# Bias of the first four tiles by 64-row matmuls, score groups as one unit, and a new order of all units in an attention and max-out kernel

## The chip, the cores and the metric

The kernel runs on one core of a Trainium2 chip. A core has engines with queues of their own: TensorE (PE, matrix multiplies, with the loads of its weights shown apart as PEld), VectorE (DVE), ScalarE (ACT), GpSimd (POOL), and SyncE (SP), which here only issues DMAs. PE reads from SBUF and writes to PSUM. Engines wait for one another through semaphores, and each works through its own list in order. The metric is the device time of one execution in microseconds (us); smaller is better.

## The reference

Attention with a local window and a few global columns, then a feed-forward layer with a maximum over three products.

```python
# q, k, v: [4, 8, 768, 64] f32; n_global = 8, n_local = 96; w1, w2, w3: [512, 768]; w_out: [768, 512]
scores = q @ k.T / sqrt(64)
rel = pos[:, None] - pos[None, :]
is_global = pos[None, :] < 8
is_local = (rel >= 0) & (rel < 96)
dist = where(is_global & ~is_local, 96, abs(rel))
slopes = 2.0 ** (-8.0 * (arange(8) + 1) / 8)            # one per head
scores = where(is_global | is_local, scores - slopes * dist, -1e9)
a = softmax(scores)
x = (a @ v) with heads side by side                     # [4 * 768, 512]
h = maximum(maximum(x @ w1, x @ w2), x @ w3)
out = h @ w_out                                         # [3072, 512]
```

## The kernel before, in words

The 3072 rows are 24 tiles of 128 positions, six to a batch. A tile T sees the keys of a window of two 64-row halves plus eight global columns; the first tile of a batch (T = 0, 6, 12, 18) sees one key set only. Everything is written as units, and the string SCHEDULE (lines 25 to 61) lists all of them in one order. A letter names the function (the table at lines 536 to 539), the numbers are its arguments, and the last one often chooses the engine. The scheduler is manual: every engine gets its instructions in the order in which the units stand in the string, and so does SP with its DMAs. Nothing else sets the order; only semaphores and free buffers decide when an instruction starts.

The life of two tiles (a pair n): l loads q (s = 0) or k (s = 1) by DMA into one of five raw buffers, c casts it to bf16, x brings it into the transposed layout qkT (how 2, 3, 6, 7, 8 by transposes on PE with copies from PSUM by ACT or DVE; 9 by a DMA transpose issued on SP). v loads values, C casts them, and Y and V copy parts of them to where tiles of odd alignment and the global rows read them. G copies the eight global key columns beside a tile's own. Then for each tile: S multiplies keys by queries for one of two groups g of four heads (8 matmuls whose contraction is 64 rows, so that two heads use the two halves of the array) and lets ACT take the exponential into P. The bias on the distance enters in one of two ways. With how = 1 two more matmuls of 128 rows first put it into PSUM, an identity times the tile "bias" (line 299), which B has made as slope times distance for each head. With how = 0 M multiplies P on DVE by the mask wmask, an exponential that K has made (line 334). Tiles 0 to 3 and one group of tile 4 take the first way, so that DVE has no masks to multiply at the start. A multiplies P by values and DVE divides by the row sum (lines 372, 373); it takes PSUM from the score buffers sp0 or sp1, or with how = 2 from the buffers "h". T transposes the result into xT, on PE with copies, or by DMA on SP (how 4). For T = 0, 6, 12, 18 a unit Z first gathers the keys of both halves into one tile kf, so that one matmul covers 128 keys.

The feed-forward part works on chunks of 4, 2, 2, 4, 4, 4 and 4 tiles. F (chunk, f, j) does four matmuls into one of three PSUM buffers "h" (line 424); for j = 0 ACT copies the result out (line 429), for j = 1 and 2 DVE takes the maximum (lines 431, 433). O multiplies by w_out and stores a tile, E does the last chunk. w, W, o and Q load and cast weights. D puts matmuls on zeros into PE's queue. Before the loop, DVE and POOL build the distance table rbq and the identity (lines 510 to 534). The first feed-forward matmul, F0.1.0, reads xT of tiles 0 to 3.

Of the kernel before, what the change touches and what calls it, by code (L numbers as in the profile page):

```python
# [12 lines left out]
FP32 = mybir.dt.float32  # L13
# [12 lines left out]
    K7 l1.0 c1.0.2 K6 l1.1 B6.1 D0.4 D4.4 B5.1 D2.0 D5.4 K0 c0.1.1 c0.0.1 K2 D8.0 B0.1 B4.0 B1.0  # L26
    B3.0 x0.1.3 K1 K3 K5 c1.1.2 B7.0 x0.0.7 D1.1 D9.2 S1.0.1 Z0.1 B2.1 v0 C0.0.2 S1.1.1 G1.0 x1.0.8
    K4 M1.0 S0.0.1 M0.0 v1 x1.1.8 S2.1.1 S2.0.1 M2.0 C0.1.2 Y0.1.2 Y1.0.1 M1.1 V2.1 Y0.0.1 G2.1 A1.2
    S0.1.1 C1.0.2 C1.1.2 Y2.0.0 Y1.1.2 D3.1 S3.0.1 M3.0 M0.1 A0.2 S3.1.1 M3.1 l2.0 c2.0.2 x2.0.6
    T1.1 M2.1 A2.0 V3.2 T0.0 G3.0 A3.1 l2.1 c2.1.2 x2.1.6 T2.1 w0.0 W0.0.0 l3.0 w0.1 S4.0.1 M4.0  # L30
    T3.8 V4.2 W0.1.2 S4.1.0 D7.1 G4.0 w0.2 F0.1.0 F0.0.0 S5.1.0 c3.0.1 x3.0.6 M4.1 w1.0 W1.0.0
    S5.0.0 F0.1.1 W0.2.2 F0.1.2 v2 C2.0.0 C2.1.0 W2.0.1 F0.0.1 F0.0.2 M5.0 F0.3.0 F0.2.0 M5.1 Y2.1.1
    V5.1 F0.5.0 w1.1 W1.1.0 W2.1.1 F0.4.0 A4.1 A5.0 F0.5.1 T4.0 F0.4.1 w1.2 W1.2.0 l3.1 T5.1 F0.2.1
    F0.2.2 l4.0 c4.0.1 W2.2.0 F0.5.2 c3.1.0 x3.1.7 Z1.0 F0.4.2 F1.0.0 F1.2.0 l4.1 c4.1.1 S7.0.0
    S6.1.0 l5.0 x4.0.6 l5.1 o0 F1.0.1 F1.0.2 c5.0.1 M7.0 F1.3.0 F1.4.0 F1.4.1 o2 c5.1.1 x4.1.7
    S6.0.0 S7.1.0 G7.0 v3 F1.2.1 F1.2.2 F1.3.1 Q2.1 F0.3.1 M7.1 Q0.0 F1.5.0 F1.5.1 S8.0.0 x5.0.7
    S8.1.0 G8.1 C3.0.2 C3.1.1 Y4.0.1 F0.3.2 F1.5.2 A7.0 F1.4.2 F1.1.0 M6.0 x5.1.6 v5 o1 Q1.0 v4
    S9.0.0 S9.1.0 l7.0 l6.1 C5.0.1 C5.1.0 F1.1.1 F1.3.2 Y3.1.1 M8.0 F1.1.2 T7.0 v6 l6.0 M6.1 v7
    Y3.0.1 M9.0 O0.2.1 l7.1 C4.0.0 O0.0.0 G9.0 V8.1 A6.1 c7.0.1 M8.1 c6.1.1 x6.1.9 O0.3.0 C4.1.0
    Y4.1.1 O0.1.1 Y5.1.0 S10.1.0 T6.8 V9.1 M9.1 S10.0.0 O1.0.0 A8.1 M10.1 T8.4 F2.0.0 x7.0.9 G10.0  # L40
    F2.4.0 c6.0.0 l8.1 v9 l9.1 F2.0.1 F2.1.0 M10.0 F2.0.2 S11.0.0 c7.1.0 Y5.0.1 x6.0.6 S11.1.0 V10.1
    F2.1.1 M11.0 F2.4.1 C6.0.0 A9.0 F2.2.0 V11.1 l9.0 O1.1.1 S13.1.0 x7.1.6 S13.0.0 G13.0 M11.1
# [14 lines left out]
    O4.1.1 A21.1 T21.4 M23.1 M22.1 O4.0.0 V22.0 F5.4.1 F5.0.0 A23.1 T23.4 O4.3.0 A22.0 F5.4.2 F5.5.2  # L57
    F5.0.1 F5.1.1 F5.0.2 T22.4 F5.1.2 F6.3.0 F6.5.0 F6.4.0 F6.5.1 F6.4.1 F6.4.2 O5.1.0 F6.3.1 F6.1.0
    O5.3.1 F6.1.1 F6.0.0 F6.0.1 F6.0.2 O5.0.1 F6.2.0 F6.2.1 F6.3.2 O5.2.0 F6.2.2 F6.1.2 F6.5.2 E
    D6.0  # L60
"""


@with_exitstack
def kernel(
# [13 lines left out]
    nc = tc.nc  # L79
# [495 lines left out]
```

## Time and profile before

| | |
|---|---|
| runs before | 176.95 us median (176.63 to 176.96, 3 runs) |
| span of the profiled execution, first to last instruction | 174.9 us; the page gives no other time of it |
| PE, DVE, ACT, POOL busy | 169.3, 132.5, 120.1, 14.3 us |
| first feed-forward matmul starts | 21.81 us |
| last matmul ends | 171.5 us |
| transposes of q and k by PE, by DMA | 14, 10 units |
| transposes of the attention output by PE, by DMA | 12, 12 units |

Busy times are sums of instructions. The ends of matmuls are modelled in the profile, so a full PE need not be at its peak. In the timeline a row gives start and length in us, engine, line, operation, output and input, and in brackets how long the engine had waited and what released it. The chain of waits is followed back from the last instruction; its rows give start, length and what ran.

### The profile page before, as it was taken

How to read it: one execution, taken by the hardware profiler on the slowest of the kernel's cores; microseconds unless marked ns; L12 is line 12 of the kernel's file. 1: busy time of each engine (PE TensorE's matmuls, PEld its weight loads, DVE VectorE, ACT ScalarE, POOL GpSimd, SP SyncE). 2: the span in 40 equal slices, each digit the busy share in tenths (PEclk: the TensorE clock that was granted, in tenths of full speed). 3: DMA queues.
4: the chain of work that ended last, by engine and by line, in shares of the span. 5: the costliest groups of instructions: out<-in, count | busy, mean ns of one | idle time of the engine just before them, and what ended most of it. 6: DMA issues, size and time to landing. Idle time of an engine off the chain costs nothing.

```text
span 174.9 us, 4233 instructions
## 1 busy us (share of the span) xinstructions
PE 169.3 (97%) x1683; PEld 93.0 (53%) x1683; DVE 132.5 (76%) x288; ACT 120.1 (69%) x188; POOL 14.3 (8%) x25
## 2 busy tenths in 40 slices
PE   6999999999999999999999999999999999999992
PEld 2445654658684587754545545544455544444451
DVE  6668859889999999998978769995569873444510
ACT  6989999789988999999948977345594413121132
POOL 5269250000100000000000000000000000000000
PEclk9999999999999999999999999999999999999999
DMA  4999999999999999976999997563101750031205
GB/s 137 347 302 335 359 350 383 385 380 312 309 282 265 298 289 228 292 213 193 257 195 185 304 233 172 166 133 60 54 10 30 105 171 0 0 119 36 89 27 213
DMA packets 55507, 35.92 MB, mean 205 GB/s; under 512 B 18368, under 2 KB 47936, under 8 KB 55488
## 3 DMA queue, kind: packets, MB, share of 16 engines
q1 hardware_dynamic: 54304, 35.07, 73.9%
q10 hardware_dynamic: 1184, 0.59, 1.3%
q8 instruction: 13, 0.21, 0.5%
q14 instruction: 6, 0.05, 0.1%
HBM read 25.17 MB, written 6.29 MB: 180 GB/s over the span
## 4 chain that ended last, share of the span: by engine, by line
PE 94%; ACT 2%; DVE 1%; issue 1%; ACTq 0%; DVEq 0%
PE h L424 53%; PE po L439 18%; PE sp L306 7%; PE op L360 6%; PE wp L504 4%; PE tpr L261 2%; PE sp L299 2%; PE xtp L411 1%; ACT qkT L268 1%; ACT wo L496 1%; PE oph L360 1%; ACT P L317 1%; PE xtr L401 0%; PE tpp L282 0%; DVE qkT L285 0%
## 5 line engine op out<-in xcount | busy, mean ns | idle before, releaser
L424 PE MATMUL h<-xT,w 128*128 128x512 bf16 (+1 forms) x504 | 100.8, 349 | 0.0
L424 PEld LDWEIGHTS <-w 128*128 128x128 bf16 x504 | 46.7, 98 | 40.7 <-ACT w L493 0.6
L317 ACT ACTIVATE P<-sp 128x1024 bf16<-128x1024 f32 (+1 forms) x48 | 44.0, 956 | 9.2 <-PE sp L306 9.1
L429 ACT CAST h<-h 128x512 bf16<-128x512 f32 (+1 forms) x42 | 21.9, 531 | 22.1 <-PE h L424 22.1
L439 PE MATMUL po<-wo,ht 128*128 128x512 bf16 (+2 forms) x156 | 34.1, 363 | 0.0
L431 DVE TENSOR_TENSOR h<-h,h 128x512 bf16<-128x512 bf16 (+1 forms) x42 | 25.2, 605 | 10.9 <-PE h L424 8.9
L433 DVE TENSOR_TENSOR ht<-h,h 128x512 bf16<-128x512 bf16 (+1 forms) x42 | 25.5, 609 | 6.3 <-PE h L424 5.0
L334 DVE TENSOR_TENSOR P<-P,wmask 128x1024 bf16<-128x1024 bf16 x33 | 22.0, 684 | 2.0 <-ACT P L317 1.9
L439 PEld LDWEIGHTS <-ht 128*128 128x128 bf16 x156 | 14.3, 98 | 15.1 <-DVE ht L433 0.2
L448 ACT COPY ost<-po 128x512 f32<-128x512 f32 (+2 forms) x16 | 8.8, 553 | 15.8 <-PE po L439 15.3
L373 DVE TENSOR_TENSOR xb<-op,rz 128x512 bf16<-128x512 f32 x22 | 15.2, 692 | 0.8
L360 PEld LDWEIGHTS <-P 128*128 128x128 bf16 x352 | 13.4, 97 | 4.4 <-issue 0.7
L306 PE MATMUL sp<-qkT 64*128 64x128 bf16 x320 | 14.3, 218 | 0.1
L306 PEld LDWEIGHTS <-qkT 64*128 64x128 bf16 x320 | 9.3, 94 | 8.2 <-issue 5.1
L448 DVE COPY ost<-po 128x512 f32<-128x512 f32 (+1 forms) x10 | 6.5, 647 | 8.4 <-PE po L439 8.4
L188 DVE CAST qkp<-rawp 128x1024 bf16<-128x1024 f32 x12 | 8.2, 687 | 1.7 <-DMA rawp<-in_k_dram 1.6
L504 PE MATMUL wp<-zeros 128*128 128x512 bf16 x17 | 7.1, 559 | 1.5 <-DVE zeros L518 1.4
L188 ACT CAST qkp<-rawp 128x1024 bf16<-128x1024 f32 x8 | 8.4, 1050 | 0.0
L268 ACT COPY qkT<-tpr 128x512 bf16<-128x512 bf16 x12 | 6.6, 588 | 1.0 <-PE tpr L261 1.0
L268 DVE COPY qkT<-tpr 128x512 bf16<-128x512 bf16 x6 | 4.0, 688 | 3.9 <-PE tpr L261 3.9
L372 DVE RECIPROCAL rz<-op 128x8 f32<-128x8 f32 x22 | 4.4, 199 | 2.5 <-PE op L360 2.3
L360 PE MATMUL op<-vo,P 128*128 128x65 bf16 x128 | 5.4, 193 | 0.3 <-issue 0.3
(84 smaller groups left out, 127.9 us busy)
## 6 DMA issues: line engine op xcount, KB each, us to landing
rawv<-in_v_dram SPq DMA_DIRECT2D x12, 512.0 KB, 7.0
out_dram<-ost SPq DMA_DIRECT2D x23, 256.0 KB, 2.4
rawp<-in_k_dram SPq DMA_DIRECT2D x8, 512.0 KB, 5.9
rawp<-in_q_dram SPq DMA_DIRECT2D x12, 256.0 KB, 5.8
wst<-in_moe_w_dram SPq DMA_DIRECT2D x3, 1024.0 KB, 11.5
rawp<-in_q_dram SPq DMA_DIRECT2D x6, 512.0 KB, 6.2
wst<-in_moe_w_dram SPq DMA_DIRECT2D x3, 512.0 KB, 8.5
rawp<-in_k_dram SPq DMA_DIRECT2D x6, 256.0 KB, 8.6
```

The costliest lines, as they stand in the source:

```text
L188: copies[how](qk, src)
L306: nc.tensor.matmul(sp[:, z, i, ds], k_cols(T, hsl, jp, ds), q_cols(T, hsl, jp), start=not how, stop=True, skip_group_check=True)
L317: nc.scalar.activation(dst, src, AF.Exp, bias=0.0, scale=scale)
L334: nc.vector.tensor_mul(P, P, wmask[:, g, :, 0:2])
L360: nc.tensor.matmul(o, P[:, i, ds], vs[ds][:, h], start=(ds == 0), stop=(ds == len(vs) - 1), skip_group_check=True)
L373: nc.vector.tensor_tensor(out=x.rearrange("p (g h) d -> p g h d", g=2), in0=o4[:, :, :, 0:64], in1=rz[:, :, :, None].to_broadcast([128, 2, ...
L424: nc.tensor.matmul(ps, w123[f // 2][:, dm, j, (f % 2) * 128:(f % 2) * 128 + 128], xT[c][:, dm], start=(dm == order[0]), stop=(dm == order[ ...
L429: nc.scalar.copy(h01, ps)
L431: nc.vector.tensor_max(h01s[c, f], h01s[c, f], ps)
L433: nc.vector.tensor_max(ht[c][:, f], h01s[c, f], ps)
L439: nc.tensor.matmul(po, ht[c][:, f, tt * 128:(tt + 1) * 128], wo[:, f, cols], start=(f == 0), stop=(f == NF - 1))
L448: copy(ost, po)
```

## The change

The bias of tiles 0 to 3 is no longer made as slope times distance. B now scales an identity of 192 columns (ident) by a head's slope into slope_id; the distance table is bf16 (rbqb), with a copy whose halves of rows are exchanged (rbqs). A group of scores gets its bias from eight matmuls of 64 rows, four on each half of the array. For T = 0, 6, 12, 18 the tile kf and the units Z are gone; each key half is now multiplied into its own half of PSUM rows by matmuls of 64 rows and 64 columns of weights. The heads of the two groups are assigned anew (group g holds heads of odd or even number). The identity is made ahead of the distance table. From tile 6 on a unit U does both score groups of a tile at once. Casts of a part may be split over two engines (how 3 to 5), loads may go out on ACT's queue, and copies of v by DMA. All v tiles are one tile vall. The string of units is new throughout.

```diff
-    K7 l1.0 c1.0.2 K6 l1.1 B6.1 D0.4 D4.4 B5.1 D2.0 D5.4 K0 c0.1.1 c0.0.1 K2 D8.0 B0.1 B4.0 B1.0
+    K1 K5 D1.8 B2.1 D3.1 K7 K6 l1.1.0 D5.6 c0.1.3 B4.1 c0.0.5 B3.0 B7.1 K0 K4 K3 B6.0 B1.2 x0.1.2
...
+SHORT = [(0, 1), (1, 1)]
...
+    ident = persist.tile([128, 192], BF16, name="ident")
+    identb = ident[:, 0:128]
...
+    rbqb = persist.tile([128, 3, 128], BF16, name="rbqb")
+    rbqs = persist.tile([128, 3, 128], BF16, name="rbqs")
+    slope_id = persist.tile([128, H, 192], BF16, name="slope_id")
...
     def short_rows(n, s):
-        return n >= 6 or (s == 1 and n < 3)
+        return n >= 6 or (n, s) in SHORT
...
+    split = ((copies[0], copies[1]), (copies[1], copies[0]), (copies[2], copies[1]))
...
+        if how >= 3:
+            for z, copy in zip(range(2), split[how - 3]):
+                if short_rows(n, s):
+                    copy(qk[:, z], src[:, z])
+                else:
+                    copy(qk[:, :, z], src[:, :, z])
+            return
...
         if how:
-
-            for hh in range(2):
-                nc.tensor.matmul(sp[:, hh, :, 0:n], identb, bias[:, g, hh, :, sets(T)],
-                                 start=True, stop=False, skip_group_check=True)
+            for i in range(2):
+                for part in range(2):
+                    for z in range(2):
+                        rows = slice(64 * z, 64 * z + 64)
+                        nc.tensor.matmul(sp[:, z, i, 0:n], slope_id[rows, 4 * z + 2 * i + g, 64 * part:64 * part + 128],
+                                         (rbqb, rbqs)[part][rows, sets(T)],
+                                         start=(i == 0 and part == 0), stop=False, skip_group_check=True)
         for ds in range(n):
             for i in range(2):
-                jp = 2 * g + i
+                jp = 2 * i + g
                 for z in range(2):
                     hsl = slice(64 * z, 64 * z + 64)
+                    if T % NT == 0:
+                        for e in range(2):
+                            nc.tensor.matmul(sp[64 * e:64 * e + 64, z, i, 0], qkT[T // NT][hsl, 1, e, jp, 0:64],
+                                             q_cols(T, hsl, jp), start=not how, stop=True, skip_group_check=True)
+                        continue
...
+    def u_U(T, how):
+        for g in range(2):
+            u_S(T, g, how)
+
     def u_B(h, how):
-        z, g, i = h // 4, h % 4 // 2, h % 2
         mul = (nc.scalar.mul, nc.vector.tensor_scalar_mul, nc.gpsimd.tensor_scalar_mul)[how]
-        mul(bias[:, g, z, i], rbq, -slopes[h] / scale)
+        mul(slope_id[:, h], ident, -slopes[h] / scale)
...
+        make_identity(nc, identb)
+        nc.vector.tensor_copy(ident[:, 128:192], ident[:, 0:64])
+        nc.gpsimd.iota(dist, base=128, pattern=[[-1, 2], [1, 2], [2, 64]], channel_multiplier=-2,
+                       allow_small_or_imprecise_dtypes=True)
...
+        for row in (0, 64):
+            nc.vector.tensor_copy(rbqs[row:row + 64], rbqb[64 - row:128 - row])
+        nc.vector.memset(heads(vall)[:, :, 64:65], 1.0)
```

Three places of the new order follow. The first is ACT's list from its first mask on, before:

```order
L326 ACTIVATE wmask<-rbq 128x384 x4
L322 ACTIVATE bias<-rbq 128x384 x3
L326 ACTIVATE wmask<-rbq 128x384 x3
L322 ACTIVATE bias<-rbq 128x384
L268 COPY qkT<-tpr 128x8x64 x2
L317 ACTIVATE P<-sp 128x1024 x2
L233 COPY qkT<-qkT 128x8x4
L326 ACTIVATE wmask<-rbq 128x384
L317 ACTIVATE P<-sp 128x4x128
```

And the same stretch of the change (qkp is a cast part, tpp and tpr are PSUM tiles of transposes, sp of scores):

```order
L345 ACTIVATE wmask<-rbqb 128x384 x4
L195 CAST qkp<-rawp 128x512
L341 ACTIVATE slope_id<-ident 128x192
L345 ACTIVATE wmask<-rbqb 128x384 x3
L341 ACTIVATE slope_id<-ident 128x192
L293 COPY qkT<-tpp 128x8x128
L276 COPY qkT<-tpr 128x8x64
L195 CAST qkp<-rawp 128x512
L333 ACTIVATE P<-sp 128x1024 x2
```

Ahead of the first exponential of scores stand the same seven masks, two scalings instead of four, and now two half casts and a copy of 1024 columns. The second place is POOL's list from the weight casts on, before to its end:

```order
L195 COPY vo_110<-vof_108 4x520
L188 CAST qkp<-rawp 128x1024
L195 COPY ve_113<-vof_108 4x520
L493 CAST w_0_117<-wst 128x4x256 x2
L191 CAST vof_109<-rawv 128x8x64
```

In the change the list goes on from its first weight cast:

```order
L512 CAST w_0_110<-wst 128x4x256
L208 COPY vall<-vall 64x520
L199 CAST qkp<-rawp 128x1024
L512 CAST w_0_110<-wst 128x4x256
L512 CAST w_2_112<-wst 128x4x256
L512 CAST w_1_111<-wst 128x4x256
L202 CAST vall<-rawv 128x8x64
L208 COPY vall<-vall 64x260 x2
L199 CAST qkp<-rawp 128x1024 x2
L202 CAST vall<-rawv 128x8x64 x2
L208 COPY vall<-vall 64x520
L208 COPY vall<-vall 4x520
```

POOL ended with one v cast after the first weights; now casts of q, k, v and weights and copies of v follow to the end of the attention part. The third place is SP's queue of DMAs behind the last load of the first weights, before:

```order
L483 DMA wst<-in_moe_w_dram 128x4x512 x2
L168 DMA rawp<-in_k_dram 128x1x512 x2
L168 DMA rawp<-in_q_dram 128x1x512 x2
L168 DMA rawp<-in_k_dram 128x1x512 x2
L168 DMA rawp<-in_q_dram 128x1x512 x2
L168 DMA rawp<-in_k_dram 128x1x512 x2
L488 DMA wost<-in_moe_w_out_dram 128x2x512 x2
```

And with the change, where the transpose of tile 5's attention output stands among the loads:

```order
L502 DMA wst<-in_moe_w_dram 128x4x512 x2
L171 DMA rawp<-in_q_dram 128x1x512 x2
L178 DMA rawv<-in_v_dram 128x8x128
L171 DMA rawp<-in_k_dram 128x1x512 x2
L400 DMA_TRANSPOSE xT<-xb 128x4x128
L507 DMA wost<-in_moe_w_out_dram 128x2x512
L171 DMA rawp<-in_q_dram 128x1x512 x2
L171 DMA rawp<-in_k_dram 128x1x512 x2
```

A load behind that transpose is issued only once tile 5's output is there. In all, 14 parts of q and k are transposed by PE as before, and of the attention output 6 tiles by PE and 18 by DMA.

More of the change, by code (lines that the diff above doesn't have):

```diff
@@ L31 @@
[L31 to L42, printed above, removed]
@@ L120 @@
     psT = ctx.enter_context(tc.tile_pool(name="psT", bufs=1, space=bass.MemoryType.PSUM))
-    identb = persist.tile([128, 128], BF16, name="identb")
+    ident = persist.tile([128, 192], BF16, name="ident")
+    identb = ident[:, 0:128]
     tiny = persist.tile([128, 1], FP32, name="tiny")
     zeros = persist.tile([128, 512], BF16, name="zeros")
-    rbq = persist.tile([128, 3, 128], FP32, name="rbq")
     shift = persist.tile([128, 1], FP32, name="shift")
@@ L193, in same @@
     def same(how, dst, src):
-        if how:
+        if how >= 3:
+            queues[how - 3].dma_start(out=dst, in_=src)
+        elif how:
             copies[how](words(dst), words(src))
```

112 lines of the change are left out of this document (56 added, 56 removed).

## The prediction

> **What bounds the kernel now.** I read the page's busy line and its chain shares first, to see which engine the time belongs to.
>
> ```profile
> PE 169.3 (97%) x1683; PEld 93.0 (53%) x1683; DVE 132.5 (76%) x288; ACT 120.1 (69%) x188; POOL 14.3 (8%) x25
> PE 94%; ACT 2%; DVE 1%; issue 1%; ACTq 0%; DVEq 0%
> ```
>
> TensorE (PE) is 97% busy and 94% of the chain. Next the busy time by stage, cut where the feed-forward matmuls begin and at changes of load (columns: stretch and length, then busy us and count of PE, weight load, DVE, ACT, POOL, then clock, DMA share, GB/s).
>
> ```profile
> 0.00:21.80 21.80, 19.63 (x271) 10.47 (x272) 16.01 (x53) 19.00 (x32) 11.27 (x22) 1.00 1.00 296
> 21.80:42.00 20.20, 20.19 (x207) 11.54 (x207) 16.63 (x30) 17.98 (x30) 2.40 (x2) 1.00 1.05 366
> 42.00:58.00 16.00, 15.96 (x206) 10.38 (x205) 15.59 (x37) 14.23 (x26) 0.62 (x1) 1.00 1.09 291
> 58.00:100.00 42.00, 42.00 (x506) 25.71 (x503) 37.93 (x87) 37.80 (x57) 0.00 (x0) 1.00 1.05 243
> ```
>
> From 21.8 on PE never rests: 20.19 of 20.20 us, then 15.96 of 16.00. A stage bounded by PE can gain only by less PE work. Before 21.8 PE is partly occupied with matmuls on zeros, and ACT works 19.00 us. Last the chain in order of time, for the ends of the two stages.
>
> ```profile
> 1.40 5.30 PE wp L504 x12
> 21.81 1.89 PE h L424 x8
> 24.48 7.01 PE h L424 x32
> 166.28 5.22 PE po L439 x36
> 171.57 0.27 ACT ost L448
> ```
>
> So the span of 174.9 us is a ramp to 21.81, PE work to 166.28 + 5.22 = 171.50 (149.69 us), and 3.4 us of last copy and store. The page gives this execution no time beyond its span; the runs' median, 176.95, is 2.05 above it, which I carry unchanged. The forecast is the ramp's new length plus the new PE work.
>
> **The ramp.** What ends it is ACT's queue, which hardly waits:
>
> ```profile
> 3.11 2.10 ACT L326 ACTIVATE wmask<-rbq 128x384 bf16<-128x384 f32 x4 [0.43 <-DVE rbq L530]
> 6.36 1.59 ACT L326 ACTIVATE wmask<-rbq 128x384 bf16<-128x384 f32 x3
> 8.27 1.04 ACT L268 COPY qkT<-tpr 128x512 bf16<-128x512 bf16 x2
> 9.80 1.94 ACT L317 ACTIVATE P<-sp 128x1024 bf16<-128x1024 f32 x2 [0.49 <-PE sp L306]
> 12.24 0.60 ACT L317 ACTIVATE P<-sp 128x512 bf16<-128x512 f32 x1
> 13.10 2.50 ACT L317 ACTIVATE P<-sp 128x1024 bf16<-128x1024 f32 x3 [0.26 <-PE sp L306]
> 18.86 0.58 ACT L412 COPY xT<-xtp 128x512 bf16<-128x512 bf16 x1
> 20.06 0.58 ACT L266 COPY qkT<-tpr 128x512 bf16<-128x512 bf16 x1 [0.37 <-PE tpr L261]
> 20.54 1.05 ACT L493 CAST w<-wst 128x1024 bf16<-128x1024 f32 x1
> 2.48 0.29 POOL masks.py:197 MEMSET identb<- 128x128 bf16 x1
> 2.84 0.33 POOL masks.py:199 TENSOR_SCALAR_AFFINE_SELECT identb<-identb 128x128 bf16<-128x128 bf16 x1
> ```
>
> From 3.11 to the end of the first weight cast, 21.59, lie 18.48 us, of which 0.49 + 0.26 + 0.37 = 1.12 are waits; 0.22 later PE starts. The change makes the identity ahead of the distance table, so POOL's 0.29 + 0.33 comes first and the exponentials that need the table start at 3.11 + 0.62 = 3.73. Then ACT's new list up to the copy of tile 3's transposed output, which the first feed-forward matmul reads. The small forms are priced by these rows:
>
> ```profile
> L191 ACT CAST vo<-rawv 128x512 bf16<-128x512 f32 x8 | 4.9, 626 | 0.0
> L322 ACT ACTIVATE bias<-rbq 128x384 bf16<-128x384 f32 x4 | 1.8, 506 | 0.0
> L233 ACT COPY qkT<-qkT 128x32 bf16<-128x32 bf16 x9 | 2.1, 231 | 0.1
> L197 ACT COPY vf<-vof 64x520 bf16<-64x520 bf16 x3 | 1.9, 619 | 0.0
> L404 ACT COPY xT<-xtr 128x256 bf16<-128x256 bf16 x1 | 0.4, 367 | 0.0
> ```
>
> Seven wmask exponentials 2.10 + 1.59 = 3.69; two scaled identities of 192 columns, between 0.23 (32) and 0.51 (384), nearest a third of the way, 2 x 0.33; two half casts 2 x 0.60; two copies of 1024, taken like a streamed exponential of that size, 2 x 1.0; three of 512, 3 x 0.52; exponentials of scores 6 x 0.97 + 2 x 0.60 = 7.02; one v copy 0.62; xT 0.37 + 2 x 0.58 = 1.53; kg copy 0.23. Sum 18.5 us. The weight cast has gone to POOL; the masks' work has not shrunk, and a 1024-wide copy that DVE made is now ACT's. With no wait PE starts at 3.73 + 18.5 + 0.22 = 22.45, with all of the old waits at 23.57. I take half of them, 0.6: at the first scores ACT now has a half cast to do while PE works, but at those of tile 2 it waits for a q copy that stands behind tile 1's four normalizing instructions on DVE. So **23.05, a loss of 1.24** (0.64 to 1.76). The 19 instead of 17 dummy matmuls cost nothing: ahead of the first transpose stand 15 x 5.30/12 = 6.6, to 8.0, and ACT takes up that transpose's result at 3.73 + 2.10 + 0.60 + 0.33 + 1.59 + 0.33 = 8.7. Without that cover, 0.3 from their transposes ending late.
>
> The new bias, eight 64-row matmuls of 256 columns per group for two 128-row ones of 512, moves the same columns twice over half the rows: 0 if halves run together as in the score rows below, +0.43 per group if not (8.90 below). It lies under ACT in the ramp; tile 4 no longer has it. The new DVE copies (rbqs, ident) end before DVE's first cast can start.
>
> **PE's work after the ramp.** Rows of the chain for each kind:
>
> ```profile
> 8.90 0.43 PE sp L299 x2
> 24.03 0.23 PE tpr L261 x16
> 39.41 0.44 PE sp L306 x12
> 52.28 0.22 PE xtp L411 x4
> 58.27 0.12 PE xtr L401 x8
> 80.05 0.55 PE sp L306 x16
> ```
>
> One q part is transposed before instead of after the first feed-forward matmul: -0.23. Of the output transposes, tiles 5, 7 and 15 (0.22 each) and 6, 9 and 10 (0.12 each) go to DMA: -1.02. Score groups of tiles 6, 12 and 18, six groups, lose the gathered kf and issue 8 matmuls of 64 columns of weights for 4 of 128. A 64-row matmul costs 0.55/16 = 0.034, two at a time; the row of 12 holds one such group of 4: 0.44 - 8 x 0.034 = 0.17. New: between 0.17, if four run at once, and 8 x 0.068 = 0.55 one at a time; no row shows a 64 by 64 matmul, and I take two at a time as in the nearest row, 8 x 0.034 = 0.28: 6 x 0.11 = +0.7 (0 to 2.3). One unit for both groups saves nothing: pairs were adjacent or had only a 64-row transpose between, and the count of breaks in the stream stays 20. Sum **-0.55** (-1.25 to +1.05). The Trainium skill, TensorEngine Tiling (Array Packing), Overview, says that 64 by 64 mode has four independent tiles; by it the 0.7 falls away. No run here shows it yet.
>
> **Waits that the new order could add.** Tile 5's output goes out by DMA and the second chunk's first matmul follows it.
>
> ```profile
> xT<-xb SPq DMA_TRANSPOSE x12, 2.5
> DMA to landing us min/median/max: 2.4/2.5/5.3
> rawp<-in_k_dram SPq DMA_DIRECT2D x6, 256.0 KB, 8.6
> L373 DVE TENSOR_TENSOR xb<-op,rz 128x512 bf16<-128x512 f32 x22 | 15.2, 692 | 0.8
> 14.23 0.59 DVE L233 COPY qkT<-qkT 128x32 bf16<-128x32 bf16 x1
> L233 DVE COPY qkT<-qkT 128x32 bf16<-128x32 bf16 x7 | 1.6, 229 | 0.1
> L188 POOL CAST qkp<-rawp 128x1024 bf16<-128x1024 f32 x4 | 4.1, 1036 | 5.4 <-DMA rawp<-in_q_dram 4.7 <-DMA rawp<-in_k_dram 0.7
> ```
>
> Between its attention and that matmul PE has 8 units of 4 x 0.219 and 1.3 of small ones, 8.3 us; less 0.9 for DVE leaves 7.4, more than the 5.3 of the slowest such DMA, but less than a load's 8.6. It is issued on SP behind the k part of tiles 8 and 9; waiting there it holds back w_out and the next q and k parts, which have about 2 us to spare. Hidden, with 1.2 at stake. POOL gets 19 instructions between 22 and 58: eight casts of 1024 columns at 1.04 and eleven of 520 and less at half of that, about 14 us for 2.40 + 0.62. That relieves DVE, which was 15.59 of 16.00 busy, of some casts, but PE did not wait for them, so this gives nothing. What it may cost: a DVE copy took 0.59 for 0.229 beside a POOL cast. I put 0.3 for all these waits (0 to 3).
>
> **Sum.** 23.05 + 149.69 - 0.55 + 0.3 + 3.4 = 175.9; + 2.05 = **177.9**, slower by 0.5%. What differs by under 0.2% (0.35 us) can't be told from no change here.
>
> **Rivals.** *Not slower: the ramp's queue closes up.* The releasers all come early: ACT waits for nothing (22.45), and the 64 by 64 groups run four at once (-1.25). Then 22.45 + 149.69 - 1.25 + 3.4 + 2.05 = 176.3. For it: before, ACT waited just 1.12 in 18.48. Against: DVE and PE hand-overs sit in the same places. It decides if the first h matmul starts by 22.4. *No change: the groups alone are free*, four at once and all else as forecast: 177.9 - 0.7 = 177.2. For it: the 64-row halves already run two at once. *Much slower: POOL blocks DVE.* About 29 DVE instructions between 22 and 58 read and write SBUF alone; met by POOL 14/36 = 0.4 of the time for half of a 1.04 cast, 29 x 0.4 x 0.4 = 4.6 us of DVE, against 36.2 - 16.63 - 15.59 = 4.0 free, and a little more for the casts that went to POOL. On PE 1 to 3 us, so 178.6 to 180.6; from about 7 us of blocking on, DVE would lead. Against it: just this one copy shows it. The Trainium skill, SBUF — State Buffer, Who interferes with whom, states an exclusive lock on the port pair that DVE and GpSimd share, the loser waiting out the whole instruction; this trace agrees, with the 0.59.
>
> **Chances.** Forecast, 177.3 to 178.6: 0.42. Much slower: 0.17. No change: 0.14. Not slower, under 176.6: 0.27. So faster 0.27, same 0.14, slower 0.59. The range 176.1 to 179.8 leaves out the ends of two rivals, about 0.1 each.
>
> **What would show it.** The first h matmul at 22.9 to 23.6, ACT at wmask from 3.7; 148.6 to 149.8 us from there to the last matmul's end; sp groups of 64 by 64 near 0.23; no idle before the h matmul behind tile 5's DMA. Wrong, if the start is under 22.4, or if PE shows stretches below full between 22 and 58: then DVE's mask and copy rows beside POOL casts should be far over their lengths in this trace.

## The result, and the profile after

The changed kernel takes 177.89 us (median of 17 runs, 176.85 to 179.13 in those compared); the kernel before took 176.82 (17 runs beside them, 176.63 to 176.96). The ratio is 1.0064, with a 95% interval of 1.0046 to 1.0082: slower by 0.6%. Executions over 1.5% above their kernel's fastest stay out of the ratios, intervals and ranges, here and below, but not out of the medians in the table: one of the change (180.00), two with x8.1 and x8.0 on TensorE, three of the kernel with three edits, and one with a k cast on DVE (181.11). The forecast was 177.9, in the range 176.1 to 179.8. The sum came out, but two of its terms were wrong and cancelled each other, as the profile shows.

The profiled execution took 177.19 us, 0.7 below the median, with a span of 175.4 (before 174.9). First the page's busy line and chain shares, then the busy time by stage, in the prediction's stretches from 21.8 on and one behind them (columns as there).

```profile
PE 167.9 (96%) x1703; PEld 94.6 (54%) x1703; DVE 129.2 (74%) x269; ACT 107.3 (61%) x169; POOL 40.9 (23%) x56
...
PE 69%; DMA 11%; ACT 7%; DVE 6%; issue 3%; SPq 1%; POOL 1%; POOLq 0%; ACTq 0%
```

```profile
21.80:42.00 20.20, 20.16 (x210) 10.63 (x209) 19.10 (x35) 16.68 (x25) 6.70 (x7) 1.00 1.09 338
42.00:58.00 16.00, 16.00 (x205) 11.74 (x204) 14.08 (x30) 13.81 (x25) 5.90 (x7) 1.00 1.23 262
58.00:100.00 42.00, 40.91 (x445) 23.83 (x443) 35.48 (x74) 27.37 (x43) 10.47 (x12) 1.00 1.08 232
100.00:140.00 40.00, 39.42 (x364) 20.51 (x365) 28.00 (x58) 24.42 (x34) 5.17 (x6) 1.00 0.81 180
```

Before, PE was 42.00 of 42.00 us busy from 58 to 100; now 40.91, and DMA, which was no part of the chain, is 11% of it. In this execution nothing is lost from 22 to 58. TensorE's timeline names the losses (the bracket is the idle time ahead of the row and its releaser).

```profile
91.53 0.31 PE L319 MATMUL sp<-qkT 64*64 64x128 bf16 x8 [0.27 <-DVE xb L392]
...
98.54 1.02 PE L443 MATMUL h<-xT,w 128*128 128x512 bf16 x4 [0.33 <-DMA xT<-xb]
...
100.52 0.62 PE L322 MATMUL sp<-qkT 64*128 64x128 bf16 x16 [0.96 <-DMA qkT<-qkp]
```

Three waits, 1.56 us: tile 18's scores wait for a buffer, chunk 4's first matmul for the output transposes of tiles 14 and 15, and the scores of tile 16 for its transposed q, x8.0. The last two come through SP's queue, which takes its items in order. Here it is ahead of them (start, time until issued).

```profile
77.20 2.38 SPq L468 DMA_DIRECT2D out_dram<-ost  x1
79.63 0.43 SPq L167 DMA_DIRECT2D rawp<-in_k_dram  x1
...
90.01 2.82 SPq L400 DMA_TRANSPOSE xT<-xb  x1
92.93 1.62 SPq L260 DMA_TRANSPOSE qkT<-qkp  x1
94.65 2.52 SPq L400 DMA_TRANSPOSE xT<-xb  x2
97.27 1.26 SPq L260 DMA_TRANSPOSE qkT<-qkp  x1
```

Tile 12's output (90.01), x8.1 (92.93), tiles 14 and 15 (94.65) and x8.0 (97.27) follow each other with no free time between, 1.3 to 2.8 us each; x8.0 lands 3.12 us after SP takes it up, when PE has waited 0.96. The kernel before has the same kinds of items here, but in an order in which nobody waits.

The ends of the two stages and x8.0's landing, from the chain in order of time:

```profile
3.55 1.93 ACT wmask L345 x4
...
21.06 0.59 ACT xT L431
...
21.70 2.32 PE h L443 x10
...
97.27 3.12 DMA qkT<-qkp
...
165.78 6.52 PE po L458 x42
```

The first feed-forward matmul starts at 21.70, 0.11 **earlier** than before. From there to 165.78 + 6.52 = 172.30 are 150.60 us; less 1.56 of waits, PE's work is 149.04, against 149.69. The end behind it is 3.1 instead of 3.4. So: -0.11 ramp, -0.65 work, +1.56 waits, -0.3 end, +0.5 in all, the difference of the spans. The other 0.7 us up to the median stand in executions that the trace does not show; the experiment on the lock finds a part of them. Another part may be the same queue: in the profiled executions of two near kernels, one with the identity made late and one with a ramp cast on DVE, the wait of 0.33 is 0.99 and 1.04.

### The profile page after: what moved, and what is told of

Its sections match the earlier page's. It is cut to its first block, busy times and chain, and to the rows that moved or that the text cites. A ratio compares the mean times of both kernels' runs of the same rounds, so it can differ in the third digit from the quotient of the medians.

```text
span 175.4 us, 4321 instructions
## 1 busy us (share of the span) xinstructions
PE 167.9 (96%) x1703; PEld 94.6 (54%) x1703; DVE 129.2 (74%) x269; ACT 107.3 (61%) x169; POOL 40.9 (23%) x56
## 4 chain that ended last, share of the span: by engine, by line
PE 69%; DMA 11%; ACT 7%; DVE 6%; issue 3%; SPq 1%; POOL 1%; POOLq 0%; ACTq 0%
PE h L443 42%; PE po L458 13%; PE sp L322 5%; DMA rawp<-in_k_dram 3%; PE op L379 3%; DMA rawv<-in_v_dram 3%; DMA rawp<-in_q_dram 3%; ACT P L333 2%; ACT wmask L345 2%; DMA qkT<-qkp 2%; PE oph L379 2%; PE tpr L269 1%; PE sp L309 1%; DVE P L353 1%; DVE vall L202 1%
## 5 line engine op out<-in xcount | busy, mean ns | idle before, releaser
L448 ACT CAST h<-h 128x512 bf16<-128x512 f32 (+1 forms) x42 | 21.5, 530 | 31.9 <-PE h L443 28.5
L353 DVE TENSOR_TENSOR P<-P,wmask 128x1024 bf16<-128x1024 bf16 x34 | 22.7, 682 | 1.8 <-ACT P L333 1.7
L199 POOL CAST qkp<-rawp 128x1024 bf16<-128x1024 f32 x15 | 17.4, 1165 | 22.1 <-DMA rawp<-in_q_dram 11.3
L202 POOL CAST vall<-rawv 128x512 bf16<-128x512 f32 x9 | 5.9, 671 | 43.3 <-DMA rawv<-in_v_dram 28.4
L322 PE MATMUL sp<-qkT 64*128 64x128 bf16 x320 | 13.4, 217 | 1.9 <-DMA qkT<-qkp 1.0
L392 DVE TENSOR_TENSOR xb<-op,rz 128x512 bf16<-128x512 f32 x17 | 11.8, 692 | 0.6
L467 DVE COPY ost<-po 128x512 f32<-128x512 f32 (+1 forms) x9 | 5.8, 644 | 8.0 <-PE po L458 8.0
L208 POOL COPY vall<-vall 4x520 int32<-4x520 int32 (+2 forms) x15 | 8.7, 577 | 7.8 <-DVE vall L208 3.9
L379 PE MATMUL op<-vall,P 128*128 128x65 bf16 x248 | 10.0, 193 | 0.0
L208 DVE COPY vall<-vall 4x520 int32<-4x520 int32 (+2 forms) x14 | 8.1, 581 | 0.9 <-ACT vall L202 0.7
L210 ACT COPY vall<-vall 64x1040 bf16<-64x1040 bf16 (+2 forms) x8 | 7.6, 948 | 1.7 <-PE op L379 1.6
```

Of the source, the lines that this page charges most:

```text
L199: copies[how](qk, src)
L208: copies[how](words(dst), words(src))
L322: nc.tensor.matmul(sp[:, z, i, ds], k_cols(T, hsl, jp, ds), q_cols(T, hsl, jp), start=not how, stop=True, skip_group_check=True)
L353: nc.vector.tensor_mul(P, P, wmask[:, g, :, 0:2])
L379: nc.tensor.matmul(o, P[:, i, ds], vs[ds][:, h], start=(ds == 0), stop=(ds == len(vs) - 1), skip_group_check=True)
L448: nc.scalar.copy(h01, ps)
```

## Experiments

Theory **queue**: the loss is PE's waiting at 90 to 101 us, made by what stands ahead on SP's queue. Rivals: **ramp** (lost before 22 us, as the prediction had it) and **lock** (GpSimd's casts hold up DVE). Where the expectations call x8.1 and x8.0, or what they load and cast, those of batch 2's first tiles, they are wrong: they are k and q of its last two, tiles 16 and 17. The times, each beside runs of the kernel before (medians 176.73 to 176.82); the kernel with split units was run once and is not in the table:

| kernel | median us, all runs | ratio to before, 95% |
|---|---|---|
| the change | 177.89 | 1.0064 (1.0046 to 1.0082) |
| x8.1 and x8.0 on TensorE | 177.04 | 1.0015 (1.0004 to 1.0025) |
| outputs of tiles 14, 15 on TensorE | 177.56 | 1.0057 (1.0032 to 1.0081) |
| casts of x8 off GpSimd | 179.98 | 1.0193 (1.0170 to 1.0216) |
| loads moved on SP | 178.58 | 1.0107 (1.0071 to 1.0142) |
| before, with 64x64 score groups | 177.56 | 1.0048 (1.0036 to 1.0060) |
| identity made late | 177.98 | 1.0081 (1.0059 to 1.0102) |
| ramp's q cast on DVE | 177.85 | 1.0062 (1.0049 to 1.0075) |
| 10 dummy matmuls for 19 | 177.49 | 1.0038 (1.0023 to 1.0053) |
| x8 on TensorE, q cast on DVE, 10 dummies | 177.38 | 1.0015 (0.9989 to 1.0040) |
| x8.1 on TensorE, 10 dummies | **176.08** | **0.9966 (0.9950 to 0.9983)** |
| one k cast on DVE | 177.42 | 1.0034 (1.0019 to 1.0049) |

### Two transposes of q and k off SP's queue

```diff
-U18.0 M18.1 c8.1.2 x8.1.9 T14.4 T15.4 M18.0 F3.0.2 c8.0.2 x8.0.9
+U18.0 M18.1 c8.1.2 x8.1.6 T14.4 T15.4 M18.0 F3.0.2 c8.0.2 x8.0.6
```

> The changed kernel, with the two transposes of batch 2's first tiles (x8.1 and x8.0, whose qkT the unit U16 needs) done by TensorE and copied by ACT and DVE, in place of two DMA transposes on SP's queue. Theory 'queue' (the 1.6 to 1.9 us of PE waits at 90 to 101 us, all of them on work that stands in SP's in-order queue, are the whole loss): PE no longer waits 0.96 us ahead of U16, and T14 and T15 stand 1.6 us earlier in the queue, so the 0.33 us ahead of chunk 4's first matmul shrinks or goes too; PE has two groups of 16 transposes more at 0.34 to 0.40 us, 0.74 us. Net -0.6 to -1.1 us against the changed kernel's 177.89: 176.8 to 177.3, ratio to the kernel before 1.000 to 1.003. Rival 'lock' (GpSimd's casts hold DVE at 86 us, which makes everything behind late): the wait moves from U16 to T14/T15 and stays 0.7 us or more; 177.6 to 178.5. Rival 'ramp' (the loss was made before 22 us): no change, plus 0.74 us of PE work: 178.6.

177.04 us. The three waits are gone from TensorE's timeline; one of 0.23 is new, at 92.91, where the second transposes wait for ACT's copy of the first. The rows of the same matmuls have no bracket now:

```profile
98.67 1.03 PE L443 MATMUL h<-xT,w 128*128 128x512 bf16 x4
99.63 0.62 PE L322 MATMUL sp<-qkT 64*128 64x128 bf16 x16
```

0.85 us came back, although TensorE has two groups of transposes more. That is what **queue** expected, and the interval lies clear of the change's; **lock** expected 177.6 or more, **ramp** 178.6.

### Two output transposes off SP's queue

```diff
-T14.4 T15.4
+T14.0 T15.0
```

> The changed kernel, with the transposes of x of tiles 14 and 15 done by TensorE (four transposes each, copied by ACT) in place of two DMA transposes on SP's queue. Theory 'queue': 2.5 us of transposes leave the queue ahead of x8.0, which is issued at about 94.7 instead of 97.27 and lands before U16 is due; chunk 4's first matmul no longer waits for a landing. Both waits (0.33 and 0.96 us, and the more in slower executions) go, PE gets 2 x 0.22 us more: -0.9 to -1.5 us against 177.89, so 176.4 to 177.0, ratio 0.998 to 1.001. Rival 'lock': T14 and T15 are late because DVE is (90.78 us for xb), so PE waits for them in its own order and the wait only changes its name: 177.6 to 178.4. Rival 'ramp': +0.45 us, 178.3.

177.56 us, no gain that can be told from the change. The waits on DMA are gone, and another has come (TensorE, then ACT):

```profile
93.48 0.38 PE L430 MATMUL xtp<-ident,xb 128*128 128x128 bf16 x4 [1.23 <-ACT xT L431]
```
```profile
91.86 1.09 ACT L333 ACTIVATE P<-sp 128x512 bf16<-128x512 f32 x2 [3.39 <-PE sp L319]
92.84 0.59 ACT L431 COPY xT<-xtp 128x512 bf16<-128x512 bf16 x1
```

Both tiles' transposes use the one buffer of the same pool. The copy that empties it stands on ACT behind two exponentials of tile 18 that can't start sooner, and PE waits 1.23 us. The expectation missed this; the queue's wait was traded for a buffer's.

### The casts off GpSimd

```diff
-c8.1.2 ... c8.0.2
+c8.1.0 ... c8.0.1
```

> The changed kernel, with the casts of batch 2's first parts (c8.1 and c8.0) moved off GpSimd: c8.1 to ACT, c8.0 to DVE. Theory 'lock' (GpSimd's two casts at 85.57, 2.76 us for two, hold DVE's two 4x520 copies, 2.44 us at 86.16 where two alone take 0.82): the copies take 0.8 us again, xb of tiles 14 and 15 come 1.0 to 1.6 us earlier (less 0.69 us for the cast that DVE has now), T14 and T15 and x8.0 behind them move forward by as much, and the PE waits at 98 to 101 us go: 176.2 to 176.9, ratio 0.996 to 1.000. Theory 'queue' alone: the order on SP is unchanged, its six items from 89 us on still follow each other at 1.3 to 2.8 us, so at most 0.5 us is gained: 177.3 to 177.9. Rival 'ramp': 177.9, no change.

179.98 us, 2.1 worse, which neither theory had forecast. The lock is there: DVE's two 4x520 copies, 2.44 us at 86.16 beside GpSimd's casts, take 0.75 without them. But that was not what held the queue.

```profile
86.15 0.75 DVE L208 COPY vall<-vall 4x520 int32<-4x520 int32 x2
```
```profile
92.38 1.05 ACT L199 CAST qkp<-rawp 128x1024 bf16<-128x1024 f32 x1
```
```profile
93.46 2.21 SPq L260 DMA_TRANSPOSE qkT<-qkp  x1
95.76 2.53 SPq L400 DMA_TRANSPOSE xT<-xb  x2
```
```profile
99.64 1.02 PE L443 MATMUL h<-xT,w 128*128 128x512 bf16 x4 [1.93 <-DMA xT<-xb]
```

On ACT the cast comes only behind tile 18's exponentials, at 92.38; GpSimd had done both by 85.57 + 2.76 = 88.33. So x8.1 holds SP to 95.7, everything behind it is 1.1 us later, and PE's wait for tiles 14 and 15 grows from 0.33 to 1.93, 1.6 of the 2.1 us. The experiment delayed one item of the queue, and the wait followed: **queue** again, by the other sign.

### Two loads moved on SP

```diff
-M13.1 F2.1.2 M14.1 G14.1 O1.0.1 l8.1 ... v8 l10.1 C9.0.1 T12.4 ... x8.0.9 v10
+M13.1 F2.1.2 M14.1 G14.1 l8.1 O1.0.1 ... v8 C9.0.1 T12.4 ... x8.0.9 l10.1 v10
```

> The changed kernel, with two loads moved on SP's queue and nothing else: the load of k for batch 2's first tiles goes ahead of an output store that waits 2.38 us for DVE (77.20), and another k load, of tiles 20 and 21, goes from ahead of tile 12's output transpose to behind x8.0. Theory 'queue' (the PE waits at 98 to 101 us come from what stands ahead on SP): the k load is issued at about 77.2 instead of 79.63, its cast and all transposes behind come 0.6 to 2 us earlier, and the waits of 0.33 and 0.96 us go: -0.8 to -1.5 us against 177.89, that is 176.4 to 177.1, ratio 0.998 to 1.002. Rival 'DMA engines full' (they are about 100% busy from 83 to 90 us, and an earlier start only lengthens every landing): less than 0.3 us gained, 177.6 to 177.9. Rival: the store comes late and holds an output buffer, so that ACT or DVE wait: 178 or more.

178.58 us (177.73 to 179.67; the profiled execution 179.21), worse than all but the last rival expected, and for another reason than that one's.

```profile
104.04 1.04 PE L443 MATMUL h<-xT,w 128*128 128x512 bf16 x4 [1.75 <-DVE xb L384]
```

The wait of 0.33 is gone and that of 0.96 is down to 0.52. But the other load, put behind x8.0, lands at 98.18 + 4.45 = 102.63; DVE, in order, waits for it with that part's cast, behind which stands tile 19's attention, and PE waits 1.75 us. Nor did the first k load gain its 2.4 us. The store ahead of it had not waited for DVE: the copy that fills it had ended at 74.01 + 0.68 = 74.69, and put behind the load it still took 2.96, the load 1.73. So the load, issued 3.2 us earlier (76.39), still landed late: its cast began 0.65 earlier, at 84.92; the DMA share is 1.08 in the change and 1.11 here from 58 to 100, so **DMA engines full**, the expectation's second theory, fits this part, though no run tests it alone.

### The kernel before, with 64 by 64 score groups

```diff
+                    if T % NT == 0:
+                        for e in range(2):
+                            nc.tensor.matmul(sp[64 * e:64 * e + 64, z, i, 0], qkT[T // NT][hsl, 1, e, jp, 0:64], ...)
+                        continue
                     nc.tensor.matmul(sp[:, z, i, ds], k_cols(T, hsl, jp, ds), q_cols(T, hsl, jp), ...)
```

> The kernel before, with one part of the change alone: the matmuls of the batches' first tiles (tiles 0, 6, 12, 18) read k straight from qkT in 64x64 quadrants, two matmuls in place of one. The copies into kf are left in, with no reader. By the prediction's price (0.28 us for a group of 16 quarter matmuls against 0.17 for the 8 before, 8 groups): +0.7 us, 177.5. By the Trainium skill's TensorEngine Tiling (four 64x64 tiles work at once): 0, so 176.8 within 0.2. If the first tiles of batches 1 to 3 waited for their kf copy, a gain of up to 0.3 us: 176.5.

177.56 us, +0.8, near the prediction's price, and not the 0 that four tiles at once would give. The chain shows where one sits; the prediction quotes the same place before as 0.44 for 12 (8 + 4), then 0.23 for the transposes.

```profile
39.67 0.33 PE sp L311 x8
40.00 0.24 PE sp L308 x8
40.24 0.34 PE tpr L261 x16
```

0.67 us became 0.91. The 64 by 64 group takes 0.24 where the kf group took 0.11 (by the starts of the rows, 39.58 and 39.69), and the transposes behind it, which are 64 rows by 128 columns, take 0.11 more than in one stream with the kf group. So the matmuls do not run one at a time (0.24 for eight, not 0.55), and each change of tile shape costs; whether they run two or four at once, 0.24 alone does not say (two at a time was priced 0.28). Over the six groups behind the ramp PE's way from first h to last po went from 149.69 to 150.32.

The other 0.26 lies in the ramp, at a pause that the profile ascribes to nothing ("issue"), first before, then here:

```profile
19.45 0.24 PE L360 MATMUL op<-vo,P 128*128 128x65 bf16 x2 [0.30 <-issue]
```
```profile
19.47 0.48 PE L365 MATMUL op<-vo,P 128*128 128x65 bf16 x10 [0.54 <-issue]
```

It stood ahead of the last 2 of 16 matmuls and now stands ahead of the last 10: 8 earlier, just as many as the edit adds ahead of it (2 groups of 4). And it ends at the same time.

### The units of tiles 6, 12 and 18 taken apart

```diff
-U6.0 M6.0 x4.0.6 F0.2.2        ... U12.0 F2.4.2        ... U18.0 M18.1 ... M18.0 F3.0.2
+S6.0.0 M6.0 x4.0.6 F0.2.2 S6.1.0 ... S12.0.0 F2.4.2 S12.1.0 ... S18.1.0 M18.1 ... F3.0.2 S18.0.0 M18.0
```

> The changed kernel with the score units of tiles 6, 12 and 18 taken apart: a feed-forward group stands between their two halves of 8 matmuls of 64 by 64. The prediction held that one unit for both halves saves nothing. If that is so, a half alone takes half of a unit's 0.35 us, about 0.18, and PE's work is unchanged. If a change of tile shape costs, as the kernel before with 64x64 groups suggests (0.23 to 0.24 us a group, and 0.09 more in the group beside it), each half takes 0.23 to 0.28: about 0.1 us more a unit, 0.3 in all, to be read from the chain's pieces, since the time of one execution does not show it.

One execution, 179.57 us. The chain has the answer, first the changed kernel, then this one:

```profile
37.66 0.35 PE sp L319 x16
```
```profile
39.41 0.24 PE sp L319 x8
...
40.96 0.24 PE sp L319 x8
```

A half alone takes 0.24, both together 0.35. So the unit saves 0.13 us for these tiles, and "saves nothing" was wrong there. The second eight add 0.35 - 0.24 = 0.11; in the kernel before, a second eight of 64 rows by 128 columns adds 0.55 - 0.33 = 0.22. So four do run at once where those run two at a time, and what a lone half loses is the change of shape.

### The ramp: identity late, a cast off GpSimd, fewer dummies

```diff
-        make_identity(nc, identb)
-        nc.vector.tensor_copy(ident[:, 128:192], ident[:, 0:64])
         nc.gpsimd.iota(dist, ...)
         ...
+        make_identity(nc, identb)
+        nc.vector.tensor_copy(ident[:, 128:192], ident[:, 0:64])
         nc.vector.memset(heads(vall)[:, :, 64:65], 1.0)
```

> The changed kernel, with the identity (and its doubled columns) made behind the distance table on GpSimd, as before the change, so that ACT's first mask exponential can start when the table is done. As the prediction has the ramp (ACT's queue from its first exponential sets the first feed-forward matmul): ACT starts 0.4 to 0.6 us earlier, at about 3.0, and the first h matmul moves from 21.70 to 21.1 to 21.3; the time falls by as much, 177.3 to 177.5. Rival: the ramp hangs on hand-overs between PE, DVE and the loads from 10.7 us on, so ACT waits longer at the first load or at the first scores and the first h matmul stays within 0.2 of 21.70: 177.7 to 178.1.

```diff
-c2.0.2
+c2.0.1
```

> The changed kernel, with one cast of the ramp (the first q part of tiles 4 and 5) moved from GpSimd to DVE, so that DVE's copy of the global keys at 14.56, 1.05 us beside that cast, takes its 0.17 to 0.2. If this one blocked copy is on the path (the chain names it, 1.06 us at 14.56): score groups of tile 2 start about 0.85 us earlier, DVE then has 0.69 us more of casting behind tile 0's attention, and the first h matmul comes 0.2 to 0.8 us earlier: 177.1 to 177.7. If PE's pause of 0.69 us at 16.61, which the profile ascribes to nothing, takes the gain up: first h matmul within 0.2 of 21.70, 177.7 to 178.1.

```diff
-D1.8 ... D5.6 ... D2.3
+D1.4 ... D5.3 ... D2.1
```

> The changed kernel, with 10 instead of 19 matmuls on zeros in the ramp (they feed nothing). As the prediction has them, they cost nothing, and without them nothing changes: first h matmul at 21.70 within 0.2, 177.7 to 178.1. Theory 'instruction count': PE's pause at 16.61 to 17.30, ascribed to nothing, stands at a fixed number of PE instructions and ends at a fixed time (in the kernel before it stood after the 14th of 16 attention matmuls and ended at 19.45; with 8 matmuls more ahead of it, after the 6th, ending at 19.47). Then it stands 9 matmuls later in the program, shrinks from 0.69 to about 0.3 us, and the first h matmul comes up to 0.4 us earlier: 177.4 to 177.7. Rival: without matmuls on zeros TensorE's granted clock is lower in the first slices and the first transposes end later: 178 or more.

With the identity late, ACT does start 0.42 earlier, and the first h matmul comes 0.64 **later**: a scaled identity that DVE makes is late for the bias matmuls.

```profile
3.13 1.93 ACT L345 ACTIVATE wmask<-rbqb 128x384 bf16<-128x384 bf16 x4 [0.44 <-DVE rbqb L551]
```
```profile
9.94 0.28 PE L309 MATMUL sp<-rbqb,slope_id 64*128 64x256 bf16 x1 [0.69 <-DVE slope_id L341]
...
22.34 2.75 PE L443 MATMUL h<-xT,w 128*128 128x512 bf16 x12
```

With the cast on DVE, the copy of the global keys takes 0.18 instead of 1.05, and the first h matmul stays at 21.75:

```profile
14.96 0.18 DVE L241 COPY qkT<-qkT 128x32 bf16<-128x32 bf16 x1 [0.88 <-PE sp L322]
```

With 9 dummies fewer, the pause of 0.69 at 16.61 to 17.30 is gone altogether, and the first h matmul is at 21.60. In these last two one chain was eased and others held the end within 0.1 us: with the cast on DVE PE's pause is still there (0.46), and with fewer dummies the chain runs through DVE's copy of the global keys, which still takes 1.03 beside GpSimd. So ACT's queue does not set the ramp alone; DVE, PE and the identities are as long. With fewer dummies the median is 0.4 lower, more than the 0.1 in the ramp, but the intervals overlap; the next point may be a part of that, which one profile can't prove. The rival of a lower clock is not settled: here the granted clock is 1.00 throughout, but the kernel with three edits below has the same 10 dummies, and in its profiled execution the clock was 0.51 from 8 to 10 us and the first h matmul came at 22.11.

### A lock that falls out one way or the other

The split kernel's execution showed something that the changed kernel's did not. DVE's mask multiplication of tile 4 and GpSimd's cast of a k part fall due together at 22.9. First the changed kernel (DVE, GpSimd), then the split one (DVE, GpSimd, TensorE):

```profile
22.81 0.68 DVE L353 TENSOR_TENSOR P<-P,wmask 128x1024 bf16<-128x1024 bf16 x1
```
```profile
22.95 1.45 POOL L199 CAST qkp<-rawp 128x1024 bf16<-128x1024 f32 x1 [1.16 <-DMA rawp<-in_k_dram]
```
```profile
22.95 1.55 DVE L353 TENSOR_TENSOR P<-P,wmask 128x1024 bf16<-128x1024 bf16 x1
```
```profile
22.92 1.04 POOL L199 CAST qkp<-rawp 128x1024 bf16<-128x1024 f32 x1 [1.20 <-PE h L443]
```
```profile
25.49 0.40 PE L322 MATMUL sp<-qkT 64*128 64x128 bf16 x8 [0.91 <-DVE qkT L241]
...
34.70 0.40 PE L430 MATMUL xtp<-ident,xb 128*128 128x128 bf16 x4 [0.42 <-DVE xb L392]
```

Whoever starts first holds the other: DVE 0.14 ahead, and the cast takes 1.45 for 1.04; the cast 0.03 ahead, and the multiplication takes 1.55 for 0.68. (With the loads moved, the cast was 0.16 ahead, 23.04 to 23.20, and the multiplication took 1.53.) In the split kernel PE then waits 0.91 + 0.42 us, and in the kernel with three edits of the next section, where the cast was 0.22 ahead, 0.85 + 0.42. With the loads moved it does not wait: DVE's copy of the global keys behind the multiplication took 0.16 there, and 1.01 in the other two, beside GpSimd's next cast. So it takes two collisions to make PE wait. The first cast's start hangs on a load's landing. So it was taken away, with one cast on DVE:

```diff
-F0.0.1 l3.1 c3.1.2
+l3.1 c3.1.1 F0.0.1
```

> The changed kernel, with one cast at 22.95 us (the k part of tiles 6 and 7) moved from GpSimd to DVE, ahead of DVE's first feed-forward maximum; TensorE and SP have the same programs. In the execution of the changed kernel DVE's mask multiplication of tile 4 began at 22.81, 0.14 us before that cast, and took 0.68, and the cast 1.45. In two other executions of near kernels the cast began 0.03 and 0.22 us before the multiplication, which then took 1.55 and 1.52; DVE's copy of global keys behind it took 1.01, and PE waited 0.91 and 0.85 us for that and 0.42 more at tile 5's transpose. Theory 'lock' (this collision, which falls out one way or the other by some hundredths of a microsecond, makes the spread of the changed kernel, 176.85 to 179.13): the median falls from 177.89 to 177.1 to 177.5, none is above 178.2, and no wait of PE between 22 and 36 shows. Rival 'queue' (the spread comes from DMA landings at 98 to 101 us): the median stays 177.6 to 178.1 and times above 178.5 still come. If DVE's added 0.69 us delays the maximum and with it PE, a wait of 0.3 to 0.7 us shows at 24 to 26: 178.2 to 178.5.

177.42 us, 0.5 less than the change; of the ten executions compared none is above 178.15 (an eleventh took 181.11, against "none is above 178.2"), and the profile shows no wait of PE between 22 and 36, while those at 98 to 101 are there (0.33 and 0.96 us). DVE:

```profile
23.48 0.17 DVE L241 COPY qkT<-qkT 128x32 bf16<-128x32 bf16 x1
23.56 0.69 DVE L199 CAST qkp<-rawp 128x1024 bf16<-128x1024 f32 x1
```

That is, but for the eleventh, as **lock** expected. The interval, 1.0019 to 1.0049, overlaps that of the change, 1.0046 to 1.0082, by a hair, so the size of the gain is not sharp. How often the collision goes the bad way in the changed kernel can't be read, since each run leaves a time only.

### A version that beats both

```diff
-c8.1.2 x8.1.9 ... D1.8 ... D5.6 ... D2.3
+c8.1.2 x8.1.6 ... D1.4 ... D5.3 ... D2.1
```

> The changed kernel with x8.1 alone on TensorE (x8.0 stays a DMA transpose) and 10 instead of 19 matmuls on zeros. Theory 'queue': one transpose of about 1.6 us less ahead of T14, T15 and x8.0 is enough; U16's wait of 0.96 us goes, T14's and T15's landing comes 1 us earlier, and PE has 0.37 us less work than with both on TensorE: 176.4 to 176.8. If one is not enough, PE waits 0.3 us or more for U16: 176.9 to 177.4.

```diff
-c2.0.2 ... c8.1.2 x8.1.9 ... x8.0.9 ... D1.8 ... D5.6 ... D2.3
+c2.0.1 ... c8.1.2 x8.1.6 ... x8.0.6 ... D1.4 ... D5.3 ... D2.1
```

> The changed kernel with three edits together: x8.0 and x8.1 on TensorE (alone 177.04, the waits of 90 to 101 us gone), the q cast of the ramp on DVE instead of GpSimd (alone 177.85, first h matmul at 21.75), and 10 instead of 19 matmuls on zeros (alone 177.49, first h matmul at 21.60, PE's pause gone). If the ramp has several chains of like length, easing DVE and PE together moves the first h matmul to 21.3 to 21.5, and the time is 176.4 to 176.8, at or just under the kernel before. If ACT's queue alone sets it, it stays at 21.6 and the time is 176.8 to 177.0.

The first takes 176.08 us, 0.34% under the kernel before and 1.8 us under the change.

```profile
58.00:100.00 42.00, 41.91 (x493) 24.92 (x492) 36.15 (x76) 28.51 (x45) 10.15 (x12) 1.00 1.13 237
100.00:140.00 40.00, 40.00 (x346) 20.23 (x343) 29.74 (x60) 23.78 (x33) 4.98 (x6) 1.00 0.77 171
```
```profile
21.40 2.75 PE L443 MATMUL h<-xT,w 128*128 128x512 bf16 x12
```

One transpose less on SP is enough: PE is busy 81.91 of 82.00 us. The ramp is 0.3 shorter, and the mask multiplication starts at 22.49, half a microsecond ahead of the cast at 23.01, so DVE wins. The second kernel, with both transposes on PE and the cast moved, has a median of 177.38 over all twelve executions and of 176.69 over the nine compared (176.16 to 178.23); by its interval it can't be told from the kernel before. The first h matmul came at 22.11 in its profiled execution, not at 21.3 to 21.5, but the clock there was 0.92 in the first 21.8 us, so its ramp is not compared. Behind the ramp that execution shows what it lost: PE's waits of 0.85 and 0.42 us from the collision of the last section, one of 0.47 for DVE at 68.55 and one of 0.24 at 95.35 for the copy between the transposes; none on DMA.

## Why the prediction was right, and where it was not

**The ramp, +1.24: wrong; it measured -0.11.** By the prediction's own sign ("wrong, if the start is under 22.4") this term is refuted, with the first h matmul at 21.70. The step that failed is the sum of ACT's list. ACT starts at 3.55, not 3.73, and is done at 21.65 with 0.73 of waits (0.18 and 0.55), near the 0.6 that were taken. So the list took 17.4 us, not 18.5. The rows show why:

```profile
6.16 1.46 ACT L345 ACTIVATE wmask<-rbqb 128x384 bf16<-128x384 bf16 x3
7.52 0.34 ACT L341 ACTIVATE slope_id<-ident 128x192 bf16<-128x192 bf16 x1
7.77 0.99 ACT L293 COPY qkT<-tpp 128x1024 bf16<-128x1024 bf16 x1
8.66 0.58 ACT L276 COPY qkT<-tpr 128x512 bf16<-128x512 bf16 x1
9.14 0.62 ACT L195 CAST qkp<-rawp 128x512 bf16<-128x512 f32 x1
```

In a row without waits the next instruction starts before the last one's end: 0.25 after a 0.34, 0.89 after a 0.99, 0.48 after a 0.58. The list summed whole durations, about 0.1 too much for each small one. And the masks, now read from a bf16 table, take 1.93 + 1.46 = 3.39 instead of 3.69, where the prediction held that they had not shrunk. That ACT ends the ramp was itself only half true, as the late identity and the missing dummies showed. Those dummies may cost something, where the prediction had nothing: without nine of them the pause is not there, and the first h matmul comes 0.1 earlier in one profiled execution and 0.3 in the other of the two that have the rest of the ramp unchanged.

**PE's work, -0.55: right in sum, -0.65 here.** The kernel with x8.1 on TensorE needs 164.03 + 6.52 - 21.40 = 149.15 us with no listed wait and one group of transposes more, so the change's own work may be nearer 148.8, -0.9. Of the terms, the fewer transposes came out: from start to start of the next row, their rows behind the ramp sum to 3.76 before and 2.67 after, -1.09 for -1.25. The +0.7 for 64 by 64 groups did not: the six sum to 1.05 before and 1.24 after, +0.2, though in the order of the kernel before the same groups cost 0.63. "One unit for both groups saves nothing" is the step that failed. The rival that they are free would have been closer in time, and not right either. The Trainium skill, TensorEngine Tiling (Array Packing), says in its Overview that 64 by 64 gives four independent tiles, which the 0.11 for eight more bears out, and in Key Properties that a change of mode drains TensorE, with which the 0.13 of a split unit agrees. The prediction weighed the first sentence and passed over the second.

**Waits, +0.3 (0 to 3): mis-sized and mis-placed.** They measured 1.56 in the profiled execution. The place watched, tile 5's output DMA, costs nothing. The mechanism was the one described there, an item on SP held behind others with landings of several us to come, but it sits at 98 to 101 us, at x8.0 and tiles 14 and 15. The prediction priced waits only up to 58 us and read no row of SP's queue behind that.

**"Much slower: POOL blocks DVE", 0.17.** In the profiled execution it is refuted from 22 to 58 us, PE 20.16 of 20.20 and 16.00 of 16.00. But the collision at 22.9 is this rival with a smaller price, up to 1.3 us of PE where it falls out badly, and without it the median is 0.5 lower, with intervals that just touch. The Trainium skill, SBUF — State Buffer, Who interferes with whom, says that the order of issue decides who blocks, and that a tensor_tensor with two SBUF inputs contends with GpSimd's reads; both rows agree.

So 177.9 was met because 1.35 us too much for the ramp stood against 1.26 too little for waits. The 0.7 by which the sum still lay above the profiled execution (0.1 of work, 0.3 at the end, 0.3 outside the span) happens to be the median's distance from that execution: luck twice. The 2.05 us outside the span set a median of runs against one execution's span; in every run on record the time lies 1.7 to 1.9 above its own span. The range held for a better reason: its ends came from rivals that are all partly here. The chance of 0.27 for faster was not idle: with one transpose moved and nine dummies dropped, the same plan is.

## What to carry to other kernels

Where work goes from an engine to DMA, list the in-order issuing queue over the whole kernel, item by item with its issue time under load, and ask which reader comes first behind the last item: the loss here sat 40 us behind the stretch that was studied. Sum a queue by its start-to-start steps, not by its durations. And before pricing a ramp by one engine, shift that engine's start by half a microsecond and see whether the end moves at all.

## What the runs showed of the hardware that was not expected

- A DMA transpose of a tile's output takes 1.2 us of SP's queue at the least (70.58 and 130.89) and up to 2.8 us with its input long there (90.01, tile 12, behind two loads just issued; its input was done at 80.6); several in a row are a wait by themselves. What makes one long is not shown: the DMA share is 0.86 at the 2.8 and 0.90 at tiles 14 and 15 with 1.26 each.
- PE pauses once in the ramp in ten of the fourteen traces, for 0.30 to 0.81 us, ascribed to nothing. It moves by 8 matmuls when 8 are added ahead of it and ends at the same time; it is gone with 9 fewer, and also with all 19 where the identity is late and PE gets there later. A 16 KB transfer on an instruction queue (13 of them in the run, 0.21 MB) starts 2.5 to 2.7 us ahead of its end in all ten traces that have the pause: at 16.9 for 19.45 before, at 14.7 for 17.30 in the change. In the four without the pause one starts at 14.4 to 15.2 too. The Trainium skill, Runtime: NRT & Kernel Launch, Instruction fetch mechanics, says that engines refill their instructions in 16 KiB blocks, mostly hidden. That this is such a refill that comes late is likely and not shown.
- A change of tile shape costs about 0.1 us on TensorE: 0.24 for eight 64 by 64 matmuls alone, 0.35 for sixteen together; they run four at once, by the 0.11 for the second eight.
- Some hundredths of a microsecond between DVE and GpSimd decide on 0.9 us: 0.68 or 1.55 for the same multiplication.
